# Rank products over the one-hot selections, GpSimd relieved of weight splits, zero stores and casts moved, in a fused retention and two-layer MoE kernel

## The chip, the cores and the metric

The kernel runs on one core of one Trainium2 chip, in one launch. Five engines work side by side, each through its own queue in order: TensorE (PE in the rows, its weight loads PEld), VectorE (DVE), ScalarE (ACT), GpSimd (POOL) and SyncE (SP), which here only issues DMAs. The metric is the device time of one execution in microseconds. Before the change the median of three runs is 439.0 us (437.39, 439.02 and 439.0).

## The reference

The program chains a retention attention and two mixture-of-experts layers, all in float32. Sizes: 2 batches, 8 heads, 768 positions, head width 64, so 1536 tokens of width 512; 8 experts with hidden width 1024; the second layer keeps at most 384 tokens per expert.

```python
# attention: per batch b and head h, over positions t
state = gamma[h] * state + outer(k[t], v[t])
y[t]  = q[t] @ state / sqrt(64)

# layer 1, on x = y as [1536, 512]
logits = x @ w_gate
e      = argmax(logits)                      # one expert per token
gate   = softmax(logits)[e]
out    = gate * (relu(x @ w1[e]) @ w2[e])

# layer 2, the same with its own weights and with a capacity:
# a token that comes later than the 384th of its expert gives zeros
```

## The kernel before

**Attention.** The tokens are cut into 12 tiles of 128 (`NT`), two per step of the state. The loop `for n in range(NT)` (line 646) is a software pipeline written out by hand: in step n it computes the masked scores of tile n (`a_scores`), the transposed, gated output of tile n-1 (`a_past`, `a_out`, which leaves `xt`), and the row form of tile n-2 with its expert logits (`comb`, through PSUM tile `cb`), which goes to DRAM as `x1d`. It issues the loads of tile n+3 on SP's queue (`a_load`: `qb`, `kt` and `vk`). The order of the calls in this loop is the order in which each engine's queue holds its work; nothing reorders it.

**Routing.** Each token's expert is the one-hot of its largest logit (`pick`). Its slot within the expert is its rank: how many earlier tokens chose the same expert. The rank comes from TensorE as two accumulated products: all-ones times the counts of the tiles before (`S`, or `run` for a batch), and a strictly lower triangular matrix `lt16` times the tile's own one-hot. `place` turns ranks into a table of token numbers. The first eight tiles are routed as two batches of four (`BATCHES`, `batch`); there DVE adds up `run` tile by tile, and TensorE multiplies all four columns at once. The last four go one by one (`route_tile`), through `step(n, i)`.

**The experts.** `layer(0, ...)` takes the experts in an order that the counts decide. For each, rows are gathered from `x1d` by an indirect DMA on GpSimd, transposed on TensorE, multiplied by both weight matrices, turned back into rows by `combine`, and scattered to `x2d` by another indirect DMA. `x2d` is filled with zeros before, by 12 stores of the tile `zero` (line 926). float32 accuracy comes from split weights: a piece of 128x1024 is loaded into `st`, ACT casts it to `whi` (`split_hi`, line 159), and DVE or GpSimd subtracts to get the rest `wlo` (`split_lo`, line 170). Each expert has eight pieces. There are four `st` buffers, so a load waits until the subtraction four pieces before it has read its buffer. Of each layer's first expert the first four pieces are used whole, without a split (`whole`), by `products`.

`between(j, i)` (line 914) is called eight times in each expert, after each quarter of the two multiplications. It refills the loads, and issues what belongs beside the products: zero stores, transposes for the next expert, waiting routing steps (`run_pend`), `split_lo` for every piece that has been cast, `split_hi` for the next. The table `POOL` says at which calls one `split_lo` goes to GpSimd instead of DVE: at i = 2 and 6 of the first seven experts of the first layer. At j = 0 a tuple of counts sets the casts of each call.

After an expert, its two row halves (the first 128 rows and the rest) are routed for layer 2 by `route_tile` in turns: `pick` of each, then `rank` of each, as entries of `pend`. The rank product of the second half uses a PSUM bank of its own (`apart`), and reads `S` after DVE has added the first half's one-hot (lines 218 and 222).

Of the kernel before, what the change touches and what calls it, by code (L numbers as in the profile page):

```python
# [18 lines left out]
P = 128  # L19
# [15 lines left out]
POOL = (((1, 5),) * (E - 1) + ((),), ((),) * E)  # L35
WARM = 40
YC = 208
WC = 1024
NST = 4
# [40 lines left out]
def fused(ctx, tc, qT, kT, vkr, wg, w11, w12, w21, w22, cst, out, capacity):  # L80
# [82 lines left out]
    def split_lo(eng=None):  # L163
        while whole(at_["lo"]) and at_["lo"] < at_["hi"]:
            at_["lo"] += 1
        q = at_["lo"]
        if q in half:
            st, hi = half.pop(q)
            lo = wp.tile([P, WC], F32R, tag="wlo", name="wlo", bufs=NW)
            (eng or V).tensor_sub(lo, st, hi)  # L170
            wq[q] = (hi, lo)
            at_["lo"] += 1


    def new_route(layer, tiles, more=0):
        st = {
            "n": 0,
            "E": cp.tile([P, tiles + more, E], F16, name=f"E{layer}"),
# [12 lines left out]
    def route_tile(rt, lg, tok, valid, cnt, last=False, at=None, apart=()):  # L191
# [23 lines left out]
        def rank():  # L215
            oh = kept["oh"]
            rk = bank("rank", "rk")[:cnt, 0:E]
            T.matmul(rk, ones16[:, :cnt], rt["S"], start=True, stop=False)
            T.matmul(rk, lt16[:cnt, :cnt], oh, start=False, stop=True)
            Et = rt["E"][:cnt, at, :]  # L220
            V.tensor_scalar(Et, oh, tok, None, ALU.mult)
            V.tensor_add(rt["S"][:cnt], rt["S"][:cnt], oh)
            ro = rp.tile([P, E], F32, tag="rro", name="rro")[:cnt]
            r = rt["r"][:cnt, at:at + 1]
            V.scalar_tensor_tensor(ro, rk, 1.0, oh, ALU.mult, ALU.mult, accum_out=r)
            R = rp.tile([P, C0], F16, tag="rR", name="rR")[:cnt]
            V.tensor_scalar(R, iota16[:cnt], r, None, ALU.is_equal)
            kept["R"], kept["E"] = R, Et
# [231 lines left out]
    run = cp.tile([P, nb + 1, E], F16, name="run")  # L460
    V.memset(run[:, 0, :], 0.0)
    rt1["S"] = run[:, nb, :]
    rt1["n"] = nb
    over = cp.tile([P, 2], F32, name="over")
    with tc.tile_pool(name="ap", bufs=3) as ap:
# [105 lines left out]
        def batch(lo, hi):  # L571
# [17 lines left out]
            def count():  # L589
                for i in range(k):  # L590
                    V.tensor_add(run[:, lo + i + 1, :], run[:, lo + i, :], kept["oh"][:, i, :])

            def rank():
                oh = kept["oh"]
                rk = pp.tile([P, k, E], F32, tag="rk", name="brk", bufs=1)
                T.matmul(rk, ones16, run[:, lo:hi, :], start=True, stop=False)
                T.matmul(rk, lt16, oh, start=False, stop=True)
# [25 lines left out]
        many = [batch(lo, hi) for lo, hi in BATCHES]  # L623
# [21 lines left out]
        G.memset(zero, 0.0)  # L645
        for n in range(NT):
            if n == first + 1:
                many[0][1]()
# [4 lines left out]
            step(n - 3, 1)  # L653
            comb(n - 2)
            if n:
                a_past(n - 1)
            if n == first + 1:
                many[0][2]()
            if n == first + 2:
                know_first = choose(rt1, 0, run[:, BATCHES[0][1], :])  # L660
# [4 lines left out]
            if n == first:  # L665
                many[0][0]()
            if first < n < first + 3:
                many[0][3](2)
            if n == second:
                many[1][0]()  # L670
                many[1][1]()
            if n:
                a_out(n - 1)
            if n == first + 3:
# [12 lines left out]
            a_load(n + 3)  # L687
            step(n - 2, 0)
# [6 lines left out]
            if n > NT - 3:  # L695
# [6 lines left out]
        def beside(i, xt):  # L702
            if i == 0:
# [3 lines left out]
                split_lo()  # L707
# [156 lines left out]
    def layer(li, xd, rin):  # L864
# [49 lines left out]
        def between(j, i):  # L914
# [9 lines left out]
            if li == 0 and j == 0:  # L924
                for t in range(NT * i // 8, NT * (i + 1) // 8):
                    nc.sync.dma_start(x2d[t * P:(t + 1) * P, :], zero)
# [6 lines left out]
            for c in range(len(half)):  # L933
                split_lo(G if c == 0 and i - 1 in POOL[li][j] else None)
            if j == 0:
                for _ in range((0, 0, 0, 1, 2, 1, 2, 1)[i]):
# [19 lines left out]
        for j in range(E):  # L956
# [40 lines left out]
            if li == 0:  # L997
# [39 lines left out]
                def rou(r, cnt, i, j=j):  # L1037
# [5 lines left out]
                    steps[r][i]()  # L1043
# [213 lines left out]
    def dropped():  # L1257
# [5 lines left out]
        route = {"S": S, "E": rp.tile([P, 1, E], F16, tag="dE", name="dE", bufs=1),  # L1263
# [147 lines left out]
```

## Time and profile before

| | |
|---|---|
| median of three runs | 439.0 us |
| profiled execution | 440.08 us, span of its instructions 438.3 us |
| TensorE busy | 409.2 us (93%) |
| DVE busy | 323.1 us (74%) |
| ACT busy | 238.5 us (54%) |
| GpSimd busy | 126.8 us (29%) |
| mean granted TensorE clock | 0.985 of 2.4 GHz |
| moved by DMA | 100.45 MB, 229 GB/s over the span |

The attention takes about the first 64 us, the first expert layer lasts until about 265 us, the second until the end. A share of busy time is a mean over these stages. The chain of work that ended last is TensorE for 54% of the span and DVE for 18%.

### The profile page before, as it was taken

How to read it: one execution, taken by the hardware profiler on the slowest of the kernel's cores; microseconds unless marked ns; L12 is line 12 of the kernel's file. 1: busy time of each engine (PE TensorE's matmuls, PEld its weight loads, DVE VectorE, ACT ScalarE, POOL GpSimd, SP SyncE). 2: the span in 40 equal slices, each digit the busy share in tenths (PEclk: the TensorE clock that was granted, in tenths of full speed). 3: DMA queues.
4: the chain of work that ended last, by engine and by line, in shares of the span. 5: the costliest groups of instructions: out<-in, count | busy, mean ns of one | idle time of the engine just before them, and what ended most of it. 6: DMA issues, size and time to landing. Idle time of an engine off the chain costs nothing.

```text
span 438.3 us, 9454 instructions
## 1 busy us (share of the span) xinstructions
PE 409.2 (93%) x3390; PEld 382.3 (87%) x3390; DVE 323.1 (74%) x863; ACT 238.5 (54%) x485; POOL 126.8 (29%) x102
## 2 busy tenths in 40 slices
PE   7999889988799999999999999999999999999980
PEld 7888669988799999999989898997888999999970
DVE  3777887368869898989898866278686878787810
ACT  2111241555657575757665742467767777778720
POOL 2434113050444535353533203003302313301120
PEclk9999999999899999999999999999999999999995
DMA  8998964788565757575756724469758677776510
GB/s 312 397 321 289 341 250 144 270 273 272 211 225 189 254 195 265 180 262 182 261 183 227 269 92 123 200 221 304 265 181 279 227 251 258 252 252 245 184 47 15
DMA packets 32503, 100.45 MB, mean 229 GB/s; under 512 B 4669, under 2 KB 5181, under 8 KB 32448
## 3 DMA queue, kind: packets, MB, share of 16 engines
q1 hardware_dynamic: 25488, 82.74, 54.1%
q0 software_dynamic: 4656, 13.00, 8.7%
q10 hardware_dynamic: 2304, 4.02, 2.4%
q8 instruction: 29, 0.48, 0.5%
q14 instruction: 26, 0.21, 0.2%
HBM read 87.01 MB, written 12.99 MB: 228 GB/s over the span
## 4 chain that ended last, share of the span: by engine, by line
PE 54%; DVE 18%; issue 10%; DMA 9%; ACT 3%; POOL 1%; SPq 1%; POOLq 0%; ACTq 0%; DVEq 0%
PE y L829 13%; PE h L785 11%; DVE wlo L170 6%; PE y L830 5%; PE h L786 5%; DMA st<-w 5%; PE h L427 4%; DMA vk<-vkr 3%; PE cb L1317 3%; DVE hs L771 2%; DVE h L797 2%; DVE rkey L205 2%; PE tp L355 2%; PE o L844 1%; PE o L846 1%
## 5 line engine op out<-in xcount | busy, mean ns | idle before, releaser
L170 DVE TENSOR_TENSOR wlo<-st,whi 128x1024 fp32r<-128x1024 f32 x107 | 139.5, 1313 | 1.0 <-ACT whi L159 1.0
L159 ACT CAST whi<-st 128x1024 fp32r<-128x1024 f32 x120 | 125.0, 1045 | 25.7 <-DMA st<-w 25.0
L829 PE MATMUL y<-h,whi 128*128 128x416 f32 (+9 forms) x384 | 117.9, 372 | 0.0
L785 PE MATMUL h<-x,whi 128*128 128x416 f32 (+9 forms) x384 | 114.5, 365 | 0.0
L830 PE MATMUL y<-h,wlo 128*128 128x208 f32 (+9 forms) x384 | 97.4, 254 | 0.0
L786 PE MATMUL h<-x,wlo 128*128 128x208 f32 (+9 forms) x384 | 96.7, 252 | 0.0
L829 PEld LDWEIGHTS y<-h,whi 128*128 128x128 f32 x384 | 72.8, 190 | 2.2 <-issue 0.2
L830 PEld LDWEIGHTS y<-h,wlo 128*128 128x128 f32 x384 | 74.1, 193 | 0.0
L785 PEld LDWEIGHTS h<-x,whi 128*128 128x128 f32 x384 | 72.1, 188 | 2.1 <-issue 0.6
L786 PEld LDWEIGHTS h<-x,wlo 128*128 128x128 f32 x384 | 73.3, 191 | 0.1
L170 POOL TENSOR_TENSOR wlo<-st,whi 128x1024 fp32r<-128x1024 f32 x13 | 34.8, 2674 | 52.3 <-ACT whi L159 52.2
L314 POOL DMA_INDIRECT out<-ob,is x14 | 15.0, 1068 | 113.2 <-ACT ob L850 110.8
L797 DVE SCALAR_TENSOR_TENSOR h<-hs,h 128x416 fp32r<-128x416 f32 (+9 forms) x48 | 27.0, 562 | 18.8 <-ACT h L796 18.3
L796 ACT ACTIVATE h<-hs 128x416 fp32r<-128x416 f32 (+9 forms) x48 | 25.1, 523 | 27.1 <-DVE hs L771 27.0
L771 DVE TENSOR_TENSOR hs<-h,hb 128x208 f32<-128x208 f32 (+9 forms) x96 | 29.7, 348 | 7.0 <-ACT hb L770 6.9
L314 POOL DMA_INDIRECT x2d<-row,is x16 | 17.1, 1069 | 60.1 <-ACT row L1330 22.9
L427 PE MATMUL h<-x,whole 128*128 128x128 f32 (+1 forms) x256 | 30.5, 277 | 0.0
L427 PEld LDWEIGHTS h<-x,whole 128*128 128x128 f32 x256 | 29.3, 192 | 0.8 <-issue 0.7
L770 ACT COPY hb<-h 128x208 f32<-128x208 f32 (+9 forms) x96 | 26.9, 318 | 4.2 <-PE h L786 4.0
L771 DVE TENSOR_TENSOR yt<-y,yb 128x208 f32<-128x208 f32 (+9 forms) x48 | 15.1, 353 | 18.0 <-ACT yb L770 18.0
L1328 ACT COPY row<-cb 128x512 f32<-128x512 f32 x11 | 6.4, 586 | 38.5 <-DVE lgb L1323 29.3
L844 PE MATMUL o<-whi,h 128*128 128x512 f32 (+1 forms) x64 | 24.3, 379 | 0.0
(195 smaller groups left out, 636.6 us busy)
## 6 DMA issues: line engine op xcount, KB each, us to landing
st<-w SPq DMA_DIRECT2D x120, 512.0 KB, 4.3
vk<-vkr SPq DMA_DIRECT2D x11, 512.0 KB, 6.1
whole<-w SPq DMA_DIRECT2D x8, 512.0 KB, 7.9
x2d<-zero SPq DMA_DIRECT2D x12, 260.0 KB, 7.7
qb<-qT SPq DMA_DIRECT2D x12, 256.0 KB, 4.5
x1d<-row ACTq DMA_DIRECT2D x11, 260.0 KB, 4.5
kt<-kT SPq DMA_DIRECT2D x11, 256.0 KB, 5.3
vk<-vkr ACTq DMA_DIRECT2D x1, 512.0 KB, 4.7
```

The costliest lines, as they stand in the source:

```text
L159: A.copy(hi, st)
L170: (eng or V).tensor_sub(lo, st, hi)
L314: ins = nc.gpsimd.indirect_dma_start(dst.rearrange("n (i d) -> (n i) d", i=parts) if parts > 1 else dst[:, :], bass.IndirectOffsetOnAxis(a ...
L427: T.matmul(ps[:, j], w[:, k, j % 2 * P:(j % 2 + 1) * P], x[:, k], start=k == 0, stop=k == KD - 1, skip_group_check=True)
L770: A.copy(b, ps[:, 1, :])
L771: V.tensor_add(out, ps[:, 0, :], b)
L785: T.matmul(ps, hi[:, k, fs], x[:, k, :, :cap], start=k == 0, stop=False, skip_group_check=True)
L786: T.matmul(ps[:, 0, :], lo[:, k, fs], x[:, k, 0, :cap], start=False, stop=k == KD - 1, skip_group_check=True)
L797: V.scalar_tensor_tensor(h[:, sl, 1, :cap], s, 0.0, h[:, sl, 0, :cap], ALU.max, ALU.subtract)
L829: T.matmul(ps[i], hi[:, ds], h[:, f, :, :cap], start=f == 0, stop=False, skip_group_check=True)
L830: T.matmul(ps[i][:, 0, :], lo[:, ds], h[:, f, 0, :cap], start=False, stop=f == KF - 1, skip_group_check=True)
L844: T.matmul(p, h[:, f, 0, ts_], hi, start=f == 0, stop=False)
```

## The change

- **Ranks.** A route keeps a list `new` of one-hots that `S` doesn't hold yet. `rank` multiplies all-ones with `S` and with each one-hot of that list, and adds them to `S` afterwards, if `more` is true. For the two halves of an expert the first half's call leaves its one-hot in the list (`more` false), and the second half's call adds both.
- **Batches.** `run` holds one column per batch instead of one per tile. `count` makes a batch's sum by one reduction, plus one addition for the second batch. `rank` of a batch multiplies all-ones with each tile's one-hot, repeated for the tiles behind it, and with the batch before.
- **Order in the attention loop.** The selection and the count of a batch come behind `a_out` instead of ahead of it. `step(n - 3, 1)`, the rank of a single tile, comes behind `comb` and `a_past`.
- **GpSimd.** The table `POOL` is gone, and DVE makes all 13 subtractions that GpSimd made.
- **Zeros.** Stores 0 to 6 of `x2d` are issued in the attention, one per step behind `a_load(n + 3)`. The other five come at the calls i = 0 (three) and i = 1 (two) of `between` in the first expert.
- **Casts.** Of the four casts at steps 10 and 11 of the attention two stay, at step 10, and one of two `split_lo` there goes. In the first expert the casts per call are (0, 1, 1, 1, 1, 2, 1, 1) instead of (0, 0, 0, 1, 2, 1, 2, 1).

```diff
-POOL = (((1, 5),) * (E - 1) + ((),), ((),) * E)
+NZ = 7
...
-    def split_lo(eng=None):
+    def split_lo():
...
-            (eng or V).tensor_sub(lo, st, hi)
+            V.tensor_sub(lo, st, hi)
...
-        def rank():
+        def rank(more=True):
             oh = kept["oh"]
+            new = rt["new"]
             rk = bank("rank", "rk")[:cnt, 0:E]
             T.matmul(rk, ones16[:, :cnt], rt["S"], start=True, stop=False)
+            for o in new:
+                T.matmul(rk, ones16[:o.shape[0], :cnt], o, start=False, stop=False)
             T.matmul(rk, lt16[:cnt, :cnt], oh, start=False, stop=True)
             Et = rt["E"][:cnt, at, :]
             V.tensor_scalar(Et, oh, tok, None, ALU.mult)
-            V.tensor_add(rt["S"][:cnt], rt["S"][:cnt], oh)
+            new.append(oh)
+            while more and new:
+                o = new.pop(0)
+                V.tensor_add(rt["S"][:o.shape[0]], rt["S"][:o.shape[0]], o)
...
             def count():
-                for i in range(k):
-                    V.tensor_add(run[:, lo + i + 1, :], run[:, lo + i, :], kept["oh"][:, i, :])
+                with nc.allow_low_precision(reason="small whole numbers"):
+                    V.tensor_reduce(run[:, at + 1, :], kept["oh"].rearrange("p k e -> p e k"), axis=AX.X, op=ALU.add)
+                if at:
+                    V.tensor_add(run[:, at + 1, :], run[:, at + 1, :], run[:, at, :])
...
-                T.matmul(rk, ones16, run[:, lo:hi, :], start=True, stop=False)
-                T.matmul(rk, lt16, oh, start=False, stop=True)
+                T.matmul(rk, lt16, oh, start=True, stop=False, skip_group_check=True)
+                if at:
+                    T.matmul(rk, ones16, run[:, at:at + 1, :].to_broadcast(sh), start=False, stop=False,
+                             skip_group_check=True)
+                for i in range(k - 1):
+                    T.matmul(rk[:, i + 1:, :], ones16, oh[:, i:i + 1, :].to_broadcast([P, k - 1 - i, E]), start=False,
+                             stop=i == k - 2, skip_group_check=True)
...
+        def clear(t):
+            nc.sync.dma_start(x2d[t * P:(t + 1) * P, :], zero)
+
         for n in range(NT):
-            if n == first + 1:
-                many[0][1]()
             a_scores(n)
             if n == NT - 1:
                 split_lo()
             a_decay(n + 1)
-            step(n - 3, 1)
             comb(n - 2)
             if n:
                 a_past(n - 1)
+            step(n - 3, 1)
...
-            if n == first:
-                many[0][0]()
...
-            if n == second:
-                many[1][0]()
-                many[1][1]()
             if n:
                 a_out(n - 1)
+            for b, m in enumerate(many):
+                if n == (first, second)[b]:
+                    m[0]()
+                    m[1]()
...
             a_load(n + 3)
+            if n < NZ:
+                clear(n)
...
-            if n > NT - 3:
+            if n == NT - 2:
                 split_hi()
                 split_hi()
...
                 step(NT - 2, 0)
-                split_lo()
...
-            if li == 0 and j == 0:
-                for t in range(NT * i // 8, NT * (i + 1) // 8):
-                    nc.sync.dma_start(x2d[t * P:(t + 1) * P, :], zero)
+            if li == 0 and j == 0 and i < 2:
+                for t in range(NZ, NT)[3 * i:3 * i + 3]:
+                    clear(t)
...
-            for c in range(len(half)):
-                split_lo(G if c == 0 and i - 1 in POOL[li][j] else None)
+            for _ in range(len(half)):
+                split_lo()
             if j == 0:
-                for _ in range((0, 0, 0, 1, 2, 1, 2, 1)[i]):
+                for _ in range((0, 1, 1, 1, 1, 2, 1, 1)[i]):
                     split_hi()
...
-                    steps[r][i]()
+                    steps[r][i](*([r == 1] if i == 1 else []))
```

## Rows read from the trace of the kernel before

**Rows 1.** Busy time by stage: stretch, its length, each engine's busy us, clock, DMA.

```profile
45.00:64.00 19.00, 15.25 (x226) 12.42 (x219) 16.41 (x73) 7.03 (x12) 2.88 (x3) 1.00 0.81 306
...
88.00:115.00 27.00, 22.25 (x143) 20.40 (x142) 21.66 (x46) 15.69 (x31) 10.10 (x6) 0.99 0.78 260
115.00:265.00 150.00, 147.21 (x1064) 141.21 (x1063) 129.16 (x374) 94.62 (x202) 59.08 (x36) 0.99 0.62 214
265.00:420.00 155.00, 154.06 (x1064) 144.05 (x1063) 111.58 (x225) 103.69 (x201) 32.61 (x28) 1.00 0.67 229
```

**Rows 2.** Timeline of TensorE, 45 to 66 us; in brackets its idle time before.

```profile
49.11 1.17 PE L1317 MATMUL cb<-iw,xt 128*128 128x136 f32 x8 [1.25 <-DVE xt L551]
...
61.48 0.63 PE L370 MATMUL tp<-cs,rows 128*128 128x128 f32 x4 [0.31 <-DMA rows<-x1d,eig]
...
63.82 0.73 PE L1348 MATMUL cb<-iw,xt 128*128 128x136 f32 x4 [1.16 <-ACT x L371]
```

**Rows 3.** Timeline of ACT, 60 to 64 us.

```profile
61.46 1.05 ACT L159 CAST whi<-st 128x1024 fp32r<-128x1024 f32 x1 [0.91 <-DMA st<-w]
...
63.39 0.65 ACT L371 COPY x<-tp 128x256 f32<-128x256 f32 x2 [0.40 <-ACT row L1328]
```

**Rows 4.** The page's costliest groups: GpSimd's share of the weight splits.

```profile
L170 POOL TENSOR_TENSOR wlo<-st,whi 128x1024 fp32r<-128x1024 f32 x13 | 34.8, 2674 | 52.3 <-ACT whi L159 52.2
```

**Rows 5.** Busy time in windows of 2 us; the last three numbers are clock, DMA share, GB/s.

```profile
18.00:20.00 2.00, 1.96 (x40) 1.79 (x42) 1.14 (x3) 0.17 (x2) 0.95 (x2) 1.00 1.05 412
...
114.00:116.00 2.00, 2.00 (x11) 1.89 (x10) 2.00 (x6) 0.00 (x0) 0.00 (x0) 0.66 0.75 270
116.00:118.00 2.00, 2.00 (x10) 1.89 (x10) 1.97 (x7) 0.98 (x3) 0.00 (x0) 0.50 0.69 254
```

**Rows 6.** Timeline of GpSimd, in the attention.

```profile
26.02 1.04 POOL L492 TENSOR_TENSOR vp<-vk,cs 128x512 f32<-128x512 f32 x1 [1.36 <-DMA vk<-vkr]
```

**Rows 7.** Timeline of TensorE, in the attention: the products of tiles 4, 5 and 6.

```profile
22.35 0.69 PE L518 MATMUL du<-vp,vk 128*64 128x64 f32 x16
...
26.65 0.69 PE L518 MATMUL du<-vp,vk 128*64 128x64 f32 x16
...
31.61 0.69 PE L518 MATMUL du<-vp,vk 128*64 128x64 f32 x16
```

**Rows 8.** Timeline of ACT, 92 to 97 us.

```profile
92.90 1.05 ACT L159 CAST whi<-st 128x1024 fp32r<-128x1024 f32 x1 [3.87 <-DMA st<-w]
...
96.35 0.59 ACT L770 COPY yb<-y 128x240 f32<-128x240 f32 x2
```

**Rows 9.** Timeline of TensorE, 92 to 120 us: its idle stretches.

```profile
97.18 0.81 PE L1317 MATMUL cb<-iw,yt 128*128 128x136 f32 x4 [1.32 <-DVE yt L771]
...
101.66 1.18 PE L1317 MATMUL cb<-iw,yt 128*112 128x136 f32 x8 [1.17 <-ACT row L1330]
...
113.19 0.21 PE L218 MATMUL rk<-S,ones 128*112 128x8 f16 x1 [2.26 <-DVE S L222]
```

**Rows 10.** DVE's groups by shape, 66 to 262 us: busy us, mean ns, idle before.

```profile
L170 DVE TENSOR_TENSOR wlo<-st,whi 128x1024 fp32r<-128x1024 f32 x49 | 69.7, 1427 | 0.0
...
L205 DVE SCALAR_TENSOR_TENSOR rkey<-row,rm,cs 128x8 f32<-128x8 f32 x8 | 1.8, 231 | 0.3
L205 DVE SCALAR_TENSOR_TENSOR rkey<-row,rm,cs 60x8 f32<-60x8 f32 x1 | 1.7, 1664 | 0.0
```

**Rows 11.** Timeline of DVE in the first layer.

```profile
110.51 2.56 DVE L221 TENSOR_SCALAR E<-roh,tk 128x8 f16<-128x8 f16 x1
...
228.12 0.54 DVE L797 SCALAR_TENSOR_TENSOR h<-hs,h 128x368 fp32r<-128x368 f32 x1
228.59 1.22 DVE L170 TENSOR_TENSOR wlo<-st,whi 128x1024 fp32r<-128x1024 f32 x1
```

**Rows 12.** TensorE's waits in the whole span: us in total, times, the longest.

```profile
PE rk L218 <- DVE S L222: 5.0, 7, 2.3
```

**Rows 13.** Timeline of TensorE, 226 to 230 us.

```profile
229.24 0.36 PE L829 MATMUL y<-h,whi 128*128 128x368 f32 x1
```

More of the change, by code (lines that the diff above doesn't have):

```diff
@@ L177, in new_route @@
             "n": 0,
+            "new": [],
             "E": cp.tile([P, tiles + more, E], F16, name=f"E{layer}"),
@@ L459, in fused @@
     nb = BATCHES[-1][1]
-    run = cp.tile([P, nb + 1, E], F16, name="run")
-    V.memset(run[:, 0, :], 0.0)
-    rt1["S"] = run[:, nb, :]
+    run = cp.tile([P, len(BATCHES) + 1, E], F16, name="run")
+    rt1["S"] = run[:, len(BATCHES), :]
     rt1["n"] = nb
@@ L569, in a_route, with batch @@
             return route_tile(rt1, lg, cs[:, tlo + n:tlo + n + 1], None, P, n == NT - 1, None, ("place",))
-        def batch(lo, hi):
+        def batch(at, lo, hi):
             k = hi - lo
@@ L621, in batch @@
             return pick, count, rank, slots, place
-        many = [batch(lo, hi) for lo, hi in BATCHES]
+        many = [batch(at, lo, hi) for at, (lo, hi) in enumerate(BATCHES)]
         a_load(0)
@@ L659, in fused @@
             if n == first + 2:
-                know_first = choose(rt1, 0, run[:, BATCHES[0][1], :])
+                know_first = choose(rt1, 0, run[:, 1, :])
             if n == second + 1:
@@ L1262, in dropped @@
         V.memset(S, 0.0)
-        route = {"S": S, "E": rp.tile([P, 1, E], F16, tag="dE", name="dE", bufs=1),
+        route = {"S": S, "new": [], "E": rp.tile([P, 1, E], F16, tag="dE", name="dE", bufs=1),
                  "r": rp.tile([P, 1], F32, tag="dr", name="dr", bufs=1)}
```

## The prediction

> **What bounds the kernel now.** I read the windows by stage first, then every idle stretch of TensorE on its own timeline, then what DVE, ACT and the loads did there. The windows [rows 1] show TensorE busy for 154.06 of 155 us in the second MoE layer, which the change doesn't touch, and for 147.21 of 150 us from 115 us on in the first. So time can be won only where TensorE stands still: 3.75 us in the attention's end (45 to 64), 4.75 us around the start of the first layer's second expert (88 to 115), 2.8 us after it, and where its clock is low. The terms below are those holes, one by one.
>
> **The attention's end.** Two of its holes end on DVE or ACT. At 49.11 TensorE waited 1.25 us for `xt`, which stood on DVE behind the second batch's selection and counts; at 63.82 it waited 1.16 us for the copies of `x` [rows 2]. The first goes with the selection behind `xt`, since TensorE needs the ranks only after the product that wanted `xt`. The second comes from ACT's queue: two casts of weights waited for their loads there, the later one started at 61.46, the row copy came behind it, and the `x` copies only at 63.39, though the transposes that they read began at 61.48 [rows 2, 3]. The change takes those two casts out of the attention, and one `split_lo` that stood on DVE ahead of the last `xt`. What is late next is the gather behind the transposes: TensorE already waited 0.31 us for it, and it hangs on a store and on weights that move by half a microsecond at most. So the 1.25 us won earlier mostly turns into waiting there. With the gather where it is, transposes at 61.48 and copies right behind them, the product at 63.82 starts at about 62.1: **1.7 us won** (estimate from these rows; nothing if the copies stay late, 2.7 if the gather comes 1 us sooner too).
>
> The two casts and the `split_lo` aren't gone, they come in `split()` at the start of the first layer: two casts on ACT, three subtractions on DVE where there were two. TensorE multiplies unsplit weights at that point (`products`), so nothing that it needs next hangs on them. I cost this at nothing; without that cover it is one cast of 1.05 us and one subtraction of 1.22 us on the path, 2.3 us [rows 3, 11].
>
> **The zeros.** Twelve stores of 260 KB wait on SP's queue in the first expert today, between the weights; seven go into the attention, one behind each tile's loads, five stay, all ahead of the next expert's fifth weight piece. SP has the loads of tile n+4 queued behind the store of step n. The attention's loads already run at 412 GB/s there, with the DMA engines full [rows 5], so each zero store delays what is behind it by about 260 KB/412 = 0.65 us. Does anybody notice? The `vk` load of tile 6 will have three of them ahead, 2.0 us. In the trace it landed at 26.02, where GpSimd took it for 1.04 us, and TensorE wanted the product of it at 31.61 [rows 6, 7]: 4.5 us of room. The tiles before it have fewer zeros ahead, and the zeros end with the seventh. I take 0; the bounds are 0 and 7 x 0.65 = 4.6 us.
>
> This is also where the Trainium skill speaks against the change. Its page "SBUF — State Buffer", section "A bandwidth-pool intuition that's wrong (but worth ruling out)", puts what HBM gives one core at about 358 GB/s. A tile's loads and stores with a zero store are 1.58 MB per step of 4.3 us (22.35 to 26.65) [rows 7], 367 GB/s, so by that figure each of the seven steps would be an estimated 0.1 us longer, 0.8 us in all; the 412 GB/s of this trace say that it doesn't apply.
>
> **The first expert and its casts.** ACT's casts of the second expert's weights stood one stage late, behind weights that came between zeros: ACT waited 3.87 us for the load at 92.90, and so took the halves of `y` only at 96.35 [rows 8]. That made TensorE wait 1.32 us at 97.18, and the pile-up behind it 1.17 us at 101.66, where ACT's row copy was late [rows 9]. With one cast per step from step 1 on, buffers come free earlier, the loads start earlier, and only five zeros lie in their way. Each cast still waits for its load, and what waits behind it on ACT is the relu of that stage; by step the loads are issued some 5 us ahead, about what they take. I take both holes as closed: **1.3 + 1.2 us**; at worst none goes and the relu waits as ACT did in [rows 8], 3.9 us.
>
> **GpSimd's splits.** Thirteen subtractions of 2.67 us leave GpSimd [rows 4] and become 13 on DVE of 1.22 us (as at 228.59) [rows 11], 15.9 us more. But DVE paid for them already: the same line's 49 subtractions take 1.43 us on average, 10 us too much in all, and a tiny `rkey` takes 1.66 us where it usually takes 0.23 (five such rows, 7.1 us together) [rows 10]; an `E` as small as that took 2.56 us beside a GpSimd split [rows 11]. Together that is some 19.5 us of DVE standing still. So DVE gets a little lighter, 0.3 us per split, and in the same place. The largest hole follows from the `E` stall: TensorE idle 2.26 us before 113.19 [rows 9], and after that the granted clock down at the lower of its two levels, 1.2 instead of 2.4 GHz: 0.66 and 0.50 over two stretches of 2 us [rows 5], 2 x (0.34 + 0.50) = 1.7 us more. Without the split neither has a cause: **2.3 + 1.7 us**.
>
> **Ranks from products.** The second half's rank product waited for the sum `S` that DVE updates after the first half's: 5.0 us in seven waits, of which 2.26 are counted above, so 2.74 in six [rows 12]. Now it needs only the two selections, which DVE made much earlier. What is late next is `h`: behind the longest of the six waits the product that uses the last `h` came at 229.24, and DVE finished that `h` at 228.66 [rows 11, 13], so 0.6 us can be won there, plus 0.3 from the lighter DVE; the other five waits are shorter than that. **2.4 us** of 2.74; lowest 0. The price is 13 more small products (eight in the layer, two and three in the batches). The row at 113.19 has 0.21 us for one [rows 9]; they overlap their neighbours, so between 0 and 0.21 each, and I take 0.1, **1.4 us lost** (0 to 2.7).
>
> **Sum.** -1.7 - 1.3 - 1.2 - 2.3 - 1.7 - 2.4 + 1.4 = -9.2 us. The profiled execution took 440.08 us (span 438.3), so 430.9; it lies 1.1 us above the median of the three runs, 439.0, and from that the forecast is **429.8 us**.
>
> **Rivals.**
> 1. *DVE stays late.* The holes close on `S` and reopen on `h`, because the added subtraction stands between one `h` and the next `hs`. For it: DVE is busy 129.16 of 150 us [rows 1]. Against: what it gains is shorter than the stall it replaces. It gives back 2.4 us and half of the 4.0: 434.2.
> 2. *The ranks don't come free.* The second product waits for something else of the first half on DVE, say the selection or a bank. Against: it writes a bank of its own kind (`apart`). Gives back the 2.4: 432.2.
> 3. *The zeros push the loads.* No room in the attention, 4.6 us later: 434.4. For it: full DMA engines; against: 4.5 us of room at tile 6.
> 4. *The casts run ahead of their loads.* The holes of 1.3 and 1.2 us stay, and relu waits 3.9: 436.2.
> 5. *Slower: DVE becomes the pace of the first layer.* If the stalls are not GpSimd's doing and stay, the 11 splits that run after 115 us put 13.4 us on a DVE that is already in order behind ACT's relu, and the 4.0 and 2.4 us aren't won: 429.8 + 6.4 + 13.4 = 449.6. It decides once DVE's 20.8 us idle in 115 to 265 can't be filled. Against: 1.66 and 2.56 us for ops of 0.23 only ever beside a split.
>
> **Chances.** Forecast 0.50, rival 1 0.18, rival 2 0.10, rival 3 0.08, rival 4 0.06, rival 5 0.05, a better case 0.03. Best end of the terms: 2.7 + 2.5 + 4.0 + 2.7 - 0 = 11.9, so 427.1, less 1.6 for the spread of the three runs: 425.5. The top takes in rivals 1 to 3: 435.5. About 2 us (0.5%) is what a measurement can tell from no change, so faster means under 436.8: forecast, rivals 1 to 3 and the better case have 0.89, less 0.03 for two rivals at once, 0.86. Within 0.5%: rival 4, at the edge, and those pairs, 0.08 (rounded down for rival 5's pairs); slower 0.06.
>
> **What would show it.** In the changed profile: no GpSimd row of the split line, `rkey` at 0.23 us everywhere, no TensorE wait on `S`, no clock below 1.0 after 113 us, the `x` copies within 0.5 us of the transposes, no cast waiting over 2 us while `y` is finished. I am wrong if TensorE's waits in the first layer move to `h` or `hs`, if its attention steps grow beyond 4.3 us, or if relu waits behind casts.

## The result, and the profile after

The changed kernel takes 428.2 us (median of four runs, 427.34 to 429.15); the kernel before took 439.0 us beside it. The ratio is 0.9756, 95% interval 0.9717 to 0.9795: faster by 10.7 us. The profiled execution took 428.34 us with a span of 426.6 us, against 440.08 and 438.3. The forecast of 429.8 us and its range hold. The path to it was partly another one: the term of the ranks belongs to another edit than the one it was booked on, the attention's came to a third in these two profiles, the price of the small products did not show, and a gain in the second layer was not foreseen.

The same instruction of both kernels is the measure for where the time went: the time between two marks on TensorE's timelines. The marks are the attention's last half product (63.82 in the kernel before, taken up again further down), the first product with `whi` that gives `y` (81.32), the first transposes of the third expert's two row halves (110.33 and 116.93), the first transposes of the second layer (250.08), the ones ahead of its first expert's second part (284.81), and those of its second expert (302.98). The last two columns are the stretch to the end of the span, and the span.

| kernel | to 81.32 | to 110.33 | to 116.93 | to 250.08 | to 284.81 | to 302.98 | to the end | span |
|---|---|---|---|---|---|---|---|---|
| before | 81.32 | 29.01 | 6.60 | 133.15 | 34.73 | 18.17 | 135.32 | 438.3 |
| changed | 80.78 | 25.94 | 3.16 | 129.87 | 34.76 | 17.24 | 134.85 | 426.6 |
| won | 0.54 | 3.07 | 3.44 | 3.28 | -0.03 | 0.93 | 0.47 | 11.7 |

The last stretch differs by up to 1.9 us from run to run, whatever the kernel (133.4 to 135.3 in the runs below), so its 0.47 is no gain to explain. The first column is hardly firmer. Splits alone and ranks alone, two kernels of the experiments below, have the same attention as the kernel before, and their first `y` comes at 82.73 and 81.76. Four profiles with the changed attention (the changed kernel twice, all but the splits, all but the ranks) have 80.69 to 81.53. The means of these groups, 81.94 and 80.97, are 1.0 us apart. The two columns behind it and the one to 250.08 repeat much better: the second run of the changed kernel has 25.96, 3.15 and 129.87.

The low clock of [rows 5] reaches past 116.93 in the kernel before, so the column to 250.08 holds a little of that, too. Counted from the next transposes, the fourth expert's (137.04), the stretch to 250.08 takes 113.04 us before and 110.30 after, 2.74 us less.

Busy time by stage of the changed kernel (length; PE, PEld, DVE, ACT, POOL in us; clock, DMA share, GB/s):

```profile
45.00:62.50 17.50, 15.48 (x234) 12.74 (x227) 14.84 (x67) 5.08 (x9) 3.78 (x4) 1.00 0.90 340
62.50:82.00 19.50, 18.46 (x174) 17.91 (x174) 14.00 (x61) 7.85 (x16) 5.98 (x5) 1.00 0.64 209
82.00:107.00 25.00, 25.00 (x168) 23.50 (x167) 20.58 (x50) 17.18 (x34) 4.55 (x4) 1.00 0.76 260
107.00:110.00 3.00, 3.00 (x24) 2.89 (x23) 2.93 (x9) 2.51 (x4) 0.00 (x0) 1.00 0.59 186
110.00:255.00 145.00, 144.99 (x1066) 139.41 (x1064) 124.95 (x378) 94.16 (x201) 32.34 (x23) 1.00 0.64 213
```

From 82 to 255 us TensorE stands still for 0.01 us and its clock is 1.00; the kernel before lost 4.75 us of idle time in 27 us and 2.79 in the next 150 [rows 1], with the low clock of [rows 5] on top. What is left of waiting lies in the attention's end and ahead of the first expert. TensorE's waits of the changed kernel, over the whole span (us in total, times, the longest), and the timeline of its idle stretches there:

```profile
PE tbp L243 <- DVE rR L234: 1.4, 2, 1.1
...
PE cb L1332 <- DVE xt L557: 0.8, 2, 0.4
PE h L434 <- ACT x L378: 0.7, 1, 0.7
...
PE btb L630 <- DVE bR L622: 0.5, 1, 0.5
PE sc L508 <- DVE xt L557: 0.5, 1, 0.5
PE tp L377 <- DMA rows<-x1d,eig: 0.3, 1, 0.3
```

```profile
57.63 0.20 PE L243 MATMUL tbp<-E,rR 128*128 128x8 f16 x2 [1.14 <-DVE rR L234]
...
61.21 0.63 PE L377 MATMUL tp<-cs,rows 128*128 128x128 f32 x4 [0.34 <-DMA rows<-x1d,eig]
...
62.24 0.71 PE L1363 MATMUL cb<-iw,xt 128*128 128x136 f32 x4
...
73.62 7.40 PE L434 MATMUL h<-x,whole 128*128 128x112 f32 x64 [0.73 <-ACT x L378]
```

There is no wait for `S` any more ([rows 12] had 5.0 us in seven). The waits of [rows 2] are gone, 1.25 us for `xt` and 1.16 us for the `x` copies; three waits of up to 0.5 us for `xt` are left. But a wait of 1.14 us for `rR` (a tile's ranks set against the slot numbers, which `place` needs) stands at 57.63, where the kernel before has 0.12; the transposes of the gathered rows start at 61.21 instead of 61.48; and a new hole of 0.73 us opens at 73.62.

On DVE the split line and `rkey`, first DVE's rows by form over the whole span (busy us, mean ns), then all `rkey` of the span (ns, shortest, median, longest):

```profile
L170 DVE TENSOR_TENSOR wlo<-st,whi 128x1024 fp32r<-128x1024 f32 x120 | 145.1, 1217 | 4.1 <-ACT x L378 2.6 <-ACT whi L159 1.6
```

```profile
L206 DVE SCALAR_TENSOR_TENSOR rkey<-row,rm,cs x20: 218/227/229, 53.8 to 252.4; 128x8 f32<-128x8 f32 x12, 112x8 f32<-112x8 f32 x1, 92x8 f32<-92x8 f32 x1, 80x8 f32<-80x8 f32 x1
```

The subtractions take 1.22 us on average now, and none more than 1.23, where the 49 of [rows 10] took 1.43, and no `rkey` takes longer than 0.229 us. DVE's busy time went from 323.1 to 319.1 us although it makes 13 subtractions more (15.9 us): what it took over it had been paying as stalls.

ACT's casts in the first expert, the timeline around the places of [rows 8]:

```profile
83.13 1.05 ACT L159 CAST whi<-st 128x1024 fp32r<-128x1024 f32 x1 [1.53 <-DMA st<-w]
...
90.90 1.05 ACT L159 CAST whi<-st 128x1024 fp32r<-128x1024 f32 x1 [1.08 <-DMA st<-w]
92.43 0.59 ACT L785 COPY yb<-y 128x240 f32<-128x240 f32 x2
```

The longest wait of a cast for its load there is 1.53 us, not 3.87, and the copies of `y` start 0.5 us behind the end of the cast at 90.90.

### The profile page after: what moved, and what is told of

Its sections match the earlier page's. It is cut to its first block, busy times and chain, and to the rows that moved or that the text cites. A ratio compares the mean times of both kernels' runs of the same rounds, so it can differ in the third digit from the quotient of the medians.

```text
span 426.6 us, 9472 instructions
## 1 busy us (share of the span) xinstructions
PE 407.3 (95%) x3403; PEld 382.0 (90%) x3403; DVE 319.1 (75%) x870; ACT 239.3 (56%) x485; POOL 96.5 (23%) x89
## 4 chain that ended last, share of the span: by engine, by line
PE 80%; DMA 9%; DVE 3%; issue 3%; SPq 1%; ACT 1%; POOL 1%; POOLq 0%; ACTq 0%; DVEq 0%
PE y L844 17%; PE h L800 17%; PE h L801 8%; PE y L845 8%; PE h L434 7%; PE cb L1332 4%; DMA vk<-vkr 3%; PE o L859 3%; PE o L861 3%; PE o L860 3%; PE tp L362 2%; DMA whole<-w 2%; DMA qb<-qT 2%; DMA rows<-x1d,eig 2%; DVE wlo L170 1%
## 5 line engine op out<-in xcount | busy, mean ns | idle before, releaser
L170 DVE TENSOR_TENSOR wlo<-st,whi 128x1024 fp32r<-128x1024 f32 x120 | 145.1, 1217 | 4.1 <-ACT x L378 2.6
L347 POOL DMA_INDIRECT rows<-x1d,igs x14 | 23.4, 1673 | 11.0 <-ACT gx L761 5.1
```

The costliest lines, as they stand in the source:

```text
L170: V.tensor_sub(lo, st, hi)
```

## The experiments

Three kernels make one edit alone on the kernel before, five take one edit back out of the changed kernel, and three more try the attention's end. In their rows `roh` is the one-hot of a row half, `E` that one-hot times the token numbers, `rkey` an early step of a selection, `hs` the sum of two partial products, and `h` on DVE the rest that rounding leaves of relu(`hs`). Theory at the start: GpSimd's splits and the casts carry the gain; the prediction had given 2.4 us of it to the ranks. Differences in us are the ratio to the kernel before times its median beside that run. The stages of the first eight, in the columns from above:

| kernel | to 81.32 | to 110.33 | to 116.93 | to 250.08 | to 302.98 less 284.81 | time against before, us (95%) |
|---|---|---|---|---|---|---|
| before | 81.32 | 29.01 | 6.60 | 133.15 | 18.17 | |
| changed | 80.78 | 25.94 | 3.16 | 129.87 | 17.24 | -10.7 (-12.4 to -9.0) |
| casts alone | 81.76 | 25.94 | 6.55 | 133.32 | 17.24 | -4.5 (-6.4 to -2.6) |
| splits alone | 82.73 | 29.22 | 3.90 | 129.96 | 18.46 | -5.6 (-8.1 to -3.1) |
| ranks alone | 81.76 | 29.27 | 6.15 | 132.71 | 18.93 | -2.5 (-3.9 to -1.1) |
| all but the casts | 83.29 | 27.58 | 3.53 | 130.17 | 17.57 | -5.4 (-7.5 to -3.2) |
| all but the splits | 81.53 | 25.92 | 3.23 | 132.25 | 17.22 | -9.2 (-10.6 to -7.9) |
| all but the ranks | 80.69 | 25.90 | 3.10 | 130.12 | 17.23 | -10.4 (-13.0 to -7.7) |
| all but the zeros | 82.90 | 25.95 | 3.65 | 130.74 | 17.24 | -11.9 (-13.5 to -10.3) |
| all but the order | 79.83 | 25.92 | 3.15 | 130.07 | 17.23 | -10.8 (-13.4 to -8.1) |

**All but the splits.** GpSimd makes its 13 subtractions again.

```diff
+POOL = (((1, 5),) * (E - 1) + ((),), ((),) * E)
...
-            for _ in range(len(half)):
-                split_lo()
+            for c in range(len(half)):
+                split_lo(G if c == 0 and i - 1 in POOL[li][j] else None)
```

> The changed kernel, with the 13 subtractions on GpSimd again; nothing else differs from the changed kernel (428.2 us). Theory: a GpSimd split holds up whatever DVE runs beside it, by 1.4 to 2.4 us, and DVE then comes late with the last h of an expert, so TensorE stands still again, most of all in the second expert, where its clock may fall; some of it is spared because the second half's rank no longer waits for the sum. I expect 430.5 to 432.5 us, rkey at 1.6 us in five places, and TensorE waits on h or hs. Rival (the whole gain of the second expert came from the ranks, GpSimd's splits are free): 428 to 429 us and no new TensorE wait over 0.5 us.

431.3 us, as expected, and six `rkey` take 1.60 to 1.67 us again. 2.4 us are lost in the stretch of the first layer's later experts, though TensorE's list has only one wait there, 0.57 us on `hs`. The stretch around the hole of [rows 9] stays short, 3.23 us. The next runs show why.

**All but the ranks.** The second half's rank product waits for the sum again.

```diff
-                    steps[r][i](*([r == 1] if i == 1 else []))
+                    steps[r][i]()
```

> The changed kernel, but the second half's rank product waits for the sum S again (the first half's selection is added at once). Theory: six or seven waits of 0.2 to 0.9 us on S return, 2 to 2.7 us in all, less some 0.1 us per product saved: 430 to 431 us. Rival (DVE without GpSimd's stalls is early enough, so the sum would be ready): under 429 us and waits on S of under 0.1 us each.

The theory missed: 428.6 us, no loss that the times can tell. Its waits on the sum, from the list of TensorE's waits:

```profile
PE rk L220 <- DVE S L229: 0.6, 2, 0.4
```

Two waits of 0.6 us in all, where the kernel before had seven of 5.0. With GpSimd out of the way the sum is nearly always early enough: from the fourth expert's first transposes on (137.04 in the kernel before) the stretch to 250.08 takes 110.54 us, 0.24 more than in the changed kernel.

**Splits alone**, on the kernel before.

```diff
-POOL = (((1, 5),) * (E - 1) + ((),), ((),) * E)
+POOL = (((),) * E, ((),) * E)
```

> The kernel before with one edit: GpSimd's 13 splits go to DVE. Theory (GpSimd's splits hold DVE up, and so cause both the hole of 2.26 us with the low clock behind it, 4.0 us in all, and the waits of the ranks for S, 2.7 us): 5 to 7 us faster than before, and no wait on S over 0.5 us although the ranks still come from the sum. Rival 1 (the S waits stand by themselves): 3 to 4.5 us faster, the six waits on S still there with about 2.7 us. Rival 2 (DVE has no room for 15.9 us more): 0 to 3 us slower.

5.4 us faster by the medians (433.9 against 439.3), in the theory's span. The waits of the rank product in this kernel, whose ranks still come from the sum:

```profile
PE rk L218 <- DVE S L222: 0.6, 2, 0.4
PE rk L218 <- DVE rro L225: 0.6, 1, 0.6
```

The wait put down to `rro`, the instruction behind `S` in DVE's queue, is what is left of the hole of [rows 9]: 0.60 us at 113.14, and no low clock behind it. So this edit alone wins 2.70 us around the hole (6.60 to 3.90) and 3.19 of the 3.28 us in the later experts; counted from 137.04 it wins 2.66 of 2.74.

**Ranks alone**, on the kernel before: the second half's list of one-hots as in the change, batches and all else as before.

```diff
+            for o in new:
+                T.matmul(rk, ones16[:o.shape[0], :cnt], o, start=False, stop=False)
...
-                    steps[r][i]()
+                    steps[r][i](*([r == 1] if i == 1 else []))
```

> The kernel before with one edit: the second half's rank product in the first layer no longer waits for the sum S (the two selections take its place). GpSimd keeps its splits. Theory (the S waits are a symptom of DVE's stalls beside GpSimd): the waits on S go, most of their 2.7 us come back on h, on the selection or on E; between 0 and 1.5 us faster than before. Rival (what my prediction said: the sum is the cause): 2 to 3 us faster, and TensorE's other waits in the first layer as before.

The time, 2.5 us (1.1 to 3.9), leans to the rival; the trace goes with the theory: the stretches in which the ranks work win 0.45 and 0.44 us (0.77 of 2.74 counted from 137.04), and the rest of this run's difference lies in the second layer's end, which varies by as much without any edit. How much above that the edit brings by itself stays open; the profiled execution took 438.69 us against a median of 437.04.

From 159.67 to 204.20 us, two experts, TensorE's timeline has neither a wait on `S` nor any other idle stretch. Even so the two take 22.20 and 22.33 us, as in the kernel before with its waits (22.32 each); in the changed kernel they take 21.81 and 21.83. What was won at the rank product is lost again in single products that start about 0.1 us late, such as the one at 161.57, right behind the end of `h` on DVE at 161.52:

```profile
161.57 0.45 PE L836 MATMUL y<-h,whi 128*128 128x400 f32 x1
```

```profile
157.16 1.64 DVE L206 SCALAR_TENSOR_TENSOR rkey<-row,rm,cs 80x8 f32<-80x8 f32 x1
...
160.94 0.58 DVE L804 SCALAR_TENSOR_TENSOR h<-hs,h 128x400 fp32r<-128x400 f32 x1
```

The hole of [rows 9] shows the same in one piece: it changed its name. TensorE, DVE and GpSimd in this kernel:

```profile
115.11 0.47 PE L836 MATMUL y<-h,whi 128*128 128x440 f32 x1 [2.02 <-DVE h L804]
```

```profile
111.21 2.93 DVE L225 TENSOR_SCALAR E<-roh,tk 128x8 f16<-128x8 f16 x1
...
114.45 0.61 DVE L804 SCALAR_TENSOR_TENSOR h<-hs,h 128x440 fp32r<-128x440 f32 x1
```

```profile
111.69 2.41 POOL L170 TENSOR_TENSOR wlo<-st,whi 128x1024 fp32r<-128x1024 f32 x1
```

The wait on `S` is gone there, but `E` stands on DVE for 2.93 us beside GpSimd's subtraction, `h` is behind it in DVE's queue, and TensorE needs `h` as well: 2.02 us instead of 2.26.

**Casts alone**, on the kernel before.

```diff
-            if n > NT - 3:
+            if n == NT - 2:
                 split_hi()
                 split_hi()
...
-                split_lo()
...
-                for _ in range((0, 0, 0, 1, 2, 1, 2, 1)[i]):
+                for _ in range((0, 1, 1, 1, 1, 2, 1, 1)[i]):
```

> The kernel before with one edit: the casts (split_hi) of the attention's last tile and the split_lo behind it go, and the first expert casts one weight per step from step 1. Zeros, GpSimd's splits and ranks as before. Theory (the casts' place on ACT makes the holes at the attention's end and the two of the first expert): 3.5 to 5.5 us faster than before; the x copies within 0.5 us of the transposes, and the holes of 1.3 and 1.2 us gone although the zeros still lie between the weights. Rival (zeros and casts make the holes together): 1 to 2.5 us faster, with casts in the first expert that wait over 2 us for loads that stand behind zeros.

4.5 us, as the theory had it; the `x` copies start 0.73 us behind the transposes, not within 0.5. The first expert's stretch takes 25.94 us, the same as with the whole change: both holes of 1.3 and 1.2 us go though 12 zeros still lie between the weights and one cast waits 2.36 us for its load. GpSimd's subtraction hits yet another instruction here, `h` itself. GpSimd, DVE, TensorE, and TensorE's clock behind it (third number from the right):

```profile
109.03 2.38 POOL L170 TENSOR_TENSOR wlo<-st,whi 128x1024 fp32r<-128x1024 f32 x1
```

```profile
108.59 3.31 DVE L796 SCALAR_TENSOR_TENSOR h<-hs,h 128x440 fp32r<-128x440 f32 x1
```

```profile
111.95 0.58 PE L828 MATMUL y<-h,whi 128*128 128x440 f32 x1 [2.13 <-DVE h L796]
```

```profile
112.00:114.00 2.00, 2.00 (x7) 1.89 (x8) 1.96 (x7) 0.03 (x1) 0.00 (x0) 0.54 0.78 242
114.00:116.00 2.00, 2.00 (x11) 1.91 (x11) 2.00 (x5) 1.63 (x4) 0.00 (x0) 0.61 0.85 225
```

Three kernels, three instructions (`E`, `E`, `h`), three names of the wait (`S`, `h`, `h`), one hole of 2.0 to 2.3 us with a clock near the lower of its levels behind it: the cause is the subtraction on GpSimd, and whichever instruction of DVE meets it. With the subtractions on DVE and nothing else changed, 0.60 us of the hole are left. In the run that has splits on GpSimd with all else changed, the subtraction fell otherwise:

```profile
103.31 3.03 POOL L171 TENSOR_TENSOR wlo<-st,whi 128x1024 fp32r<-128x1024 f32 x1 [0.15 <-ACT whi L160]
112.82 2.40 POOL L171 TENSOR_TENSOR wlo<-st,whi 128x1024 fp32r<-128x1024 f32 x1 [6.48 <-ACT whi L160]
```

Nothing runs on GpSimd between 106.4 and 112.8, when `E` and `h` are due at 107.92 and 108.65, and the hole does not come. That is one reason why taking the splits back out costs only 1.5 us by the ratios, 2.7 by the spans, while they win 5.6 alone.

The Trainium skill, page "SBUF — State Buffer", section "Who interferes with whom", says that a DVE instruction with two SBUF inputs and a GpSimd instruction that reads SBUF lock each other out completely, not by shares of bandwidth, and that the one issued first has its way. The first half agrees: `h`, with two inputs, ends at 111.90 beside a subtraction that ends at 111.41, and takes 3.31 us instead of 0.61. The order does not: by the records `h` started 0.44 us before the subtraction, and still was the one held up.

**All but the casts.**

```diff
-            if n == NT - 2:
+            if n > NT - 3:
                 split_hi()
                 split_hi()
...
+                split_lo()
...
-                for _ in range((0, 1, 1, 1, 1, 2, 1, 1)[i]):
+                for _ in range((0, 0, 0, 1, 2, 1, 2, 1)[i]):
```

> The changed kernel, but the casts as before: four in the attention, two split_lo there, and counts (0,0,0,1,2,1,2,1) in the first expert. Theory: the x copies of the attention's end are late again by 1.2 to 1.6 us, but the gather of the second rows and its copies hide most of that, so by the first y product only 0.5 us is lost; in the first expert the casts stand one call late, and with fewer zeros in the way TensorE waits 0 to 1.5 us for yt: 428.7 to 430.2 us. Rival (the casts' times are the cause of both holes at 97 and 101 us): 430.7 us or more.

The rival's time was right: 434.2 us, 5.3 us of the gain gone. TensorE's idle stretches in it, and the cast of the first expert that waits longest for its load:

```profile
62.48 0.63 PE L377 MATMUL tp<-cs,rows 128*128 128x128 f32 x4 [1.37 <-DMA rows<-x1d,eig]
64.89 0.73 PE L1364 MATMUL cb<-iw,xt 128*128 128x136 f32 x4 [1.23 <-ACT x L378]
...
102.20 1.18 PE L1333 MATMUL cb<-iw,yt 128*112 128x136 f32 x8 [1.17 <-ACT row L1346]
```

```profile
95.36 1.05 ACT L159 CAST whi<-st 128x1024 fp32r<-128x1024 f32 x1 [1.99 <-DMA st<-w]
```

The wait for the `x` copies at the attention's end is back with 1.23 us and the second hole of the first expert with 1.17. The first hole, 1.32 us in [rows 9], is not: the casts wait 1.29 and 1.99 us for their loads, where the one of [rows 8] waited 3.87. Splits alone and ranks alone still have that wait with 4.08 and 4.12 us and the hole with 1.52 and 1.59. So with the old casts one of the other edits closes the first hole, most likely the zeros, since the order belongs to the attention; no run has the zeros alone.

**All but the zeros.**

```diff
-            if n < NZ:
-                clear(n)
...
-            if li == 0 and j == 0 and i < 2:
-                for t in range(NZ, NT)[3 * i:3 * i + 3]:
-                    clear(t)
+            if li == 0 and j == 0:
+                for t in range(NT * i // 8, NT * (i + 1) // 8):
+                    clear(t)
```

> The changed kernel, but all 12 zero stores go out in the first expert again, spread over its eight calls as before. Theory: the loads of the second expert's weights land late behind zeros, ACT waits for them and TensorE waits 1 to 1.3 us for yt and again for the next row copy: 2 to 3 us more, 430.2 to 431.2 us, and the attention's steps as in the changed kernel (4.3 us) since seven zeros cost nothing there. Rival (the casts' order made the gain, not the zeros): within 0.7 us of 428.2 us; rival (zeros do cost time in the attention): faster there by 1 us or more up to 60 us.

Missed: 429.0 us, and the first expert's stretch is as short (25.95). With the new casts, where the zeros are stored costs nothing that the times can tell. (Its profiled execution took 432.1 us, the longest of four: the gathered rows came at 62.33 after a wait of 2.67 us, and that shows in the first column. Two casts wait 2.08 and 1.34 us for their loads, and the two stretches behind the first expert are 0.5 and 0.9 us longer than in the changed kernel; whether these belong to the zeros stays open.)

**All but the order.** Selection ahead of `xt`, rank step ahead of `comb`.

```diff
-            comb(n - 2)
-            if n:
-                a_past(n - 1)
             step(n - 3, 1)
+            comb(n - 2)
+            if n:
+                a_past(n - 1)
```

(and the loop over `many` back ahead of `a_out`)

> The changed kernel with the attention's order of before: a batch's selection stands ahead of xt on DVE again, and the rank step ahead of comb. Theory (what the order wins in the attention is lost again at the gather, whose rows land no sooner): within 0.5 us of the changed kernel (428 to 429), with a wait for xt of some 1.2 us at the attention's last tile, and the first expert's first y product within 0.5 us of where it was. Rival (the order is worth what it removes): 1 to 1.7 us slower than the changed kernel.

428.1 us: the order brings nothing that the times can tell. With the wait for `xt` back (0.91 us) the transposes of the gathered rows start at 61.22, against 61.21; and this run is the one of all changed ones that has no hole at 73.62, so that its first `y` comes at 79.83, 0.95 us sooner than in the changed kernel.

**Three tries at the attention's end**, beside a second run of the changed kernel: the rank step alone back; the half products of the last tile, which its routing needs, ahead of the transposes of the gathered rows; and these with the old order.

```diff
-                rt1["x"] = first_x(rt1["rows"])
                 way.half(0, mmtile("ca"), last[0])
...
                 way.half(1, mmtile("cb"), xt)
+                rt1["x"] = first_x(rt1["rows"])
```

> The changed kernel once more, as the measure for the three runs beside it: 427.5 to 429.0 us, with the same hole of 0.7 us before the second half's first products (x copies late) and the first expert's first y product at 80.8.

> The changed kernel with half of the attention's order of before: the rank step stands ahead of comb again, the selection stays behind xt. Theory (the rank step behind comb and a_past makes the ranks late, 1.1 us of waiting for rR, and shifts the x copies): the waits for rR under 0.5 us, the hole of 0.7 us gone, the first y product at 79.8 to 80.2, 427 to 428 us. Rival (the selection behind xt does it): both stay, the first y product at 80.8.

> The changed kernel with one edit: the last tile's half products, from which its routing follows, stand ahead of the transposes of the gathered rows, so routing no longer waits for the gather. Theory (the gather's landing at 61 caps the attention's end, and the chain behind it sets when the next rows can be fetched): 1.0 to 1.5 us faster than the changed kernel, the half product starts at 61 instead of 62.2, the next gather goes out 1 us sooner, and fewer warm products run before its rows are there. Rival (DVE's last xt or the x copies come no sooner): within 0.4 us of the changed kernel.

> Both: the attention's order of before (selection ahead of xt, rank step ahead of comb) and the half products ahead of the gathered rows' transposes. Theory: the two add up, 2.0 to 2.5 us faster than the changed kernel, the first y product at about 78.5. Rival (both draw on the same wait for the gather): no better than the half products alone.

The changed kernel again: 427.9 us. Step back: 427.95; halves first: 427.9; both: 429.4. None is faster than the change, and the theories of the last three missed. In the first, the wait for `rR` went but the hole did not (0.68 us). In the second, TensorE's timeline shows the half product no sooner, waiting for `xt`, behind DVE:

```profile
62.84 0.73 PE L1363 MATMUL cb<-iw,xt 128*128 128x136 f32 x4 [0.16 <-DVE xt L557]
63.40 0.60 PE L377 MATMUL tp<-cs,rows 128*128 128x128 f32 x4
64.51 1.16 PE L434 MATMUL h<-x,whole 128*128 128x128 f32 x8 [0.48 <-ACT x L378]
```

In the changed kernel the gathered rows are there at 61.21 and DVE's last `xt` ends at 61.75. So DVE's chain from the last tiles and the gather end within about half a microsecond of each other, and moving one behind the other won nothing.

## Why the prediction was right, and where its steps were not

- **Attention's end, 1.7 us forecast: 0.54 in these two profiles, 1.0 between the means of all that have either attention.** The mechanism of the `x` copies holds: transposes to half product takes 1.03 us instead of 2.34, and 1.07 with the casts alone. The bound that the prediction named, the gather, holds too: what the order won at `xt` turned into the wait for `rR` and the gather. What it missed is behind the mark it reckoned to: the half product came 1.58 us sooner, at 62.24 (62.1 was forecast), but 1.04 us of it are lost by the first `y`, 0.31 in a second wait for `rR` at 63.26 and 0.73 in the hole at 73.62, where the `x` copies of the second rows started at 73.22, 1.8 us behind their transposes. The row credits a product on TensorE; why the copies wait for it stays open. The hole came in every kernel made from the changed one but one, with the old order too (both, 0.67 us), and in none of the three with a single edit.
- **Zeros, 0: right for the attention.** None of the 4.6 us of the upper bound came: the `du` products of tile 7, behind all seven zeros, start at 36.05 in both kernels. In the first expert the new casts close both holes without them; with the old casts one of the other edits, most likely the zeros, closes the first.
- **First expert's holes, 2.5: 3.07.** The casts alone bring all of it; with all but the casts 1.43 us of it are there as well, so the two causes overlap. The same edit brings the unforeseen 0.93 us in the second layer: the step from 284.81 to 302.98 is 17.22 to 17.26 us in every run with the new casts and 17.57 to 18.93 in every run without. The kernel before waits there for rows (its timeline):

```profile
302.98 0.63 PE L355 MATMUL tp<-cs,rows 128*128 128x128 f32 x4 [0.79 <-DMA rows<-x2d,igs]
```

  The gather for them stands on GpSimd behind a scatter, and that behind ACT's `ob`, which comes right behind a cast that waited for its load (ACT's timeline):

```profile
294.29 1.05 ACT L159 CAST whi<-st 128x1024 fp32r<-128x1024 f32 x1 [0.82 <-DMA st<-w]
295.24 0.68 ACT L850 ACTIVATE ob<-o,gt 128x512 f32<-128x512 f32 x1
```

  That is 10.4 us after the transposes at 284.81; with the casts alone `ob` comes 8.5 us after them. The prediction had called the second layer untouched, but the code reads the tuple of casts at `j == 0` of either layer, so the change moves the casts of the second layer's first expert, too.
- **GpSimd's hole and the clock, 4.0: 3.44**, of which the splits alone bring 2.70, and 0.54 more from 116.93 to the next transposes, the stretch in which the low clock ended. The mechanism was right. The clock is 1.00 over all of 110 to 255.
- **Ranks, 2.4: the step that failed.** The 2.74 us from 137.04 on are there, but splits alone bring 2.66 of them, ranks alone 0.77, and all but ranks keeps 2.50. The prediction took the wait for `S` at its name and priced the dependence; `S` was only the last thing in a DVE queue held up by GpSimd. Rival 1, that the waits would go over to `h`, is what happens when the ranks change and the splits stay; without the splits on GpSimd there is next to nothing left to go over.
- **Small products, 1.4 lost: next to nothing.** With the eight products of the layer the stretch to 250.08 is 129.87 us, without them 130.12, of which 0.51 are waits on `S`. Each has 0.17 to 0.19 us in the trace, but on the timeline of the changed kernel the next product follows 0.04 us behind it.
- **DVE as the pace (rival 5): no.** It is busy 124.95 of 145 us, the same share as 129.16 of 150.

By the prediction's marks: no `S` wait, no low clock, `rkey` at 0.23, no cast waiting over 2 us, the first `x` copies 0.45 us behind their transposes: all seen. The 1.8 us of the second `x` copies were the one miss. The total came out because the holes were real ones and the change closes them, whichever of its edits does it. That it came out so near is partly luck: the spans differ by 11.7 us where the sum had 9.2. The attention's 1.2 us too much were made up by 1.4 us for products that cost next to nothing, and 0.9 us in the second layer, 0.6 more in the first expert and 0.5 in the last stretch were in no term.

## What to carry to other kernels

Where a consumer waits for a tiny result on a busy engine, look first at what its queue held just before: if a short instruction there takes several times its usual time, ask what ran beside it. Here removing the dependence only gave the hole another name. An engine that takes over work which it was already paying for in stalls need not get slower: DVE's busy time fell by 4.0 us. When edits overlap, make each alone and take each back out: here the ranks look worth 2.5 us by themselves and nothing beside the others, and either the casts or another edit closes the first expert's first hole. And look whether code that is meant for one stage runs in another, too, as the tuple of casts does.

## What the runs showed of the hardware

- One subtraction of 128x1024 on GpSimd (2.4 to 3.0 us in the kernel before) held up DVE instructions of 0.2 to 0.6 us beside it by 1.4 to 2.7 us: `rkey` took 1.66 us, `E` 2.56 and 2.93, `h` 3.31. In the runs without these subtractions the longest `rkey` is 0.229 us.
- The records suggest that it goes the other way as well, in a small way. With all subtractions on DVE the instruction with which GpSimd issues a gather took up to 2.63 us, against 1.87 in the first layer of the kernel before, while DVE ran `h`, a subtraction and `hs` back to back. No run tests this by itself. From GpSimd's timeline of the changed kernel:

```profile
125.42 1.18 POOL L347 DMA_INDIRECT rows<-x1d,igs  x1 [0.30 <-issue]
126.91 2.62 POOL L347 DMA_INDIRECT rows<-x1d,igs  x1 [0.31 <-issue]
```

  Nobody waits for these rows, so it costs nothing here.
- After each of the three holes of 2.0 to 2.3 us in the first layer the granted clock stood at 0.50 to 0.66 for the next two windows of 2 us, near 1.2 of 2.4 GHz; the holes of 1.3 and 1.2 us in [rows 9] have no such stretch behind them (1.00 from 96 to 108).
- The same happened in the attention, and there the length of the last hole does not decide it. Splits alone, casts alone and ranks alone waited 2.12, 2.06 and 1.75 us for `xt` at about 50 us, and the clock stood at 0.50 from 52 to 54; the kernel before waited 1.25 us there and had 1.00. The kernel with the step back had it at 0.50 behind two waits of no more than 0.53 and 0.87 us, at 52.48 and 55.53. Windows of splits alone, then of the kernel with the step back:

```profile
52.00:54.00 2.00, 2.00 (x30) 1.63 (x24) 1.06 (x6) 1.60 (x3) 0.00 (x0) 0.50 1.05 420
```

```profile
56.00:58.00 2.00, 2.00 (x16) 1.75 (x19) 2.00 (x6) 0.00 (x0) 0.46 (x1) 0.50 1.02 411
```
